# Matmul operands of a fused attention and two-MLP kernel started 4 to 56 bytes into their SBUF slots

## The chip, the cores and the metric

The kernel runs on one core of one Trainium2 chip. The metric is device time in microseconds of one execution. The kernel before takes 1527.72 us, the median of two runs (1527.64 and 1527.79 us).

## The reference

Three stages follow each other. `_attn_ref` packs 576 keys and values of each of 8 batches and 8 heads into 32 rows by a softmax attention, and lets the 576 queries attend to those 32 rows. `_moe_ref` and `_moe2_ref` are two dense MLPs over all 4608 tokens, 512 wide with 2048 hidden units.

```python
def _attn_ref(q, k, v, p):            # (8, 8, 576, 64); p has 32 rows
    p_packed = sm_attn(p, k, v)
    out = sm_attn(q, p_packed, p_packed)
    return out.astype(np.float32)

def _moe_ref(x, w_in, w_out):
    h = x @ w_in
    g = np.where(h > 0.0, h, alpha * (np.exp(np.minimum(h, 0.0)) - 1.0))
    return (g @ w_out).astype(np.float32)

def _moe2_ref(x, w_in, w_out, a, b):
    h = x @ w_in
    P = a[0] + a[1] * h + a[2] * h2 + a[3] * h3
    Q = 1.0 + np.abs(b[0]) * np.abs(h) + np.abs(b[1]) * h2
    g = P / (Q + 1e-06)
    return (g @ w_out).astype(np.float32)
```

## The kernel before

The order of the work is written out by hand, step by step, in the main loops at the end of the kernel function; the engines run their instructions in that order. There are two phases.

Phase A (lines 935 to 963) does attention and the first MLP. The tokens are taken as 8 batches of two halves of 288 tokens, and each half takes 16 steps, one for each 128 hidden units: 256 steps. The second attention isn't finished as such. Its softmax weights, transposed, are the tile `A` (two heads' rows, one half), and `m` is the packed values times the first MLP's `w_in`, so that `h` is `m` times `A`. Every number is split into a high and a low part of type float32r, and a product is taken as three matmuls (high by high, low by high, high by low). In a step, `a_h` (L358) issues 6 matmuls of 288 columns whose moving operand is a slice of `A`; ScalarE and VectorE make `g` (L376, L377, L382); `a_hi` (L387, ScalarE) and `a_lo` (L392, VectorE) split it into `ghi` and `glo`; `a_o` (L402) issues 12 matmuls whose moving operand is `ghi` or `glo`, into four accumulators. The stationary operands there are `m` and `wo`. The tile `A` is written by `s2_hi` (L311, ScalarE) and `s2_lo` (L316, VectorE) from `s2y`, which `s2_tr` (L305, VectorE) transposes. Attention of the next batch and the unpacking of the weights run between the steps. The result of the first MLP goes to DRAM (`x2d`).

Phase B (lines 966 to 999) does the second MLP over 9 blocks of 512 tokens, 16 steps each: 144 steps. `b_load` (L611, the DMAs of L616 on SP's queue) brings a block's x, high and low, as two tiles `xb` of 1 MB each; two blocks are held at a time, and a block is loaded while the one before it is worked on. In a step, `b_h` (L631) issues 12 matmuls of 512 columns whose moving operand is `xb` (stationary: the weights `w`); ScalarE and VectorE work out the rational function (L645 to L668); `b_split` makes `ghi` (L674, ScalarE) and `glo` (L676, GpSimd); `b_o` (L684) issues 12 matmuls in which `ghi` or `glo` is the stationary operand and `wo` the moving one.

Tiles come from pools with slots by tag. In the kernel before, the built program has every matmul operand, moving and stationary, at an SBUF address that is a multiple of 64 bytes.

Of the kernel before, what the change touches and what calls it, by code (L numbers as in the profile page):

```python
# [10 lines left out]
F32 = mybir.dt.float32  # L11
F32R = mybir.dt.float32r
# [10 lines left out]
def packed_attention_moe_moe2_kernel(  # L23
# [15 lines left out]
    B, _, NJ, S = qT.shape  # L39
# [5 lines left out]
    NF = DFF // 128  # L45
    NC = DFF // 512
    TA = S // 2
    NBLK = TA // 32
    TB = 512
    NTB = NT // TB  # L50
    NKD = DM // 128
# [10 lines left out]
    WI = (1, 2, 3, 4, 7, 8, 9, 10, 11, 12, 13, 14)  # L62
    SCH = (6, 8, 11, 13, 14), (18, 24), (20, 22, 26, 30)
    NWS = NF - 1

    P = ctx.enter_context(tc.tile_pool(name="P", bufs=1))
    dram = ctx.enter_context(tc.tile_pool(name="dram", bufs=1, space=bass.MemoryType.DRAM))
# [2 lines left out]
    T = actx.enter_context(tc.tile_pool(name="T", bufs=1))  # L70
# [230 lines left out]
    def s2_tr(b, hf):  # L301
        d = st[b]
        x, m = d.pop(("s2x", hf))
        y = T.tile([128, 2, TA], F32, tag="s2y", name=f"s2y_{b}_{hf}")
        nc.vector.transpose(y.rearrange("p a s -> p (a s)"), x.rearrange("p a s -> p (a s)"))  # L305
        d["s2y", hf] = y

    def s2_hi(b, hf):
        d = st[b]
        d["A", hf] = A = T.tile([128, 2, 2, TA], F32R, tag="A", name=f"A_{b}_{hf}", bufs=tag_bufs["A"])  # L310
        nc.scalar.copy(A[:, 0], d["s2y", hf])  # L311

    def s2_lo(b, hf, eng=None):
# [4 lines left out]
    tag_bufs = dict(A=3, raw=2, cvt=2, E=2, aT=2)  # L318
# [27 lines left out]
    def a_step(s):  # L346


        b, t = divmod(s, 2 * NF)
        if b == 0:  # L350
            for n, f0, f1 in RUNS:
                if t < f1 - f0:
                    return b, n, f0 + t, (t == 0, t == f1 - f0 - 1)
                t -= f1 - f0
        n, f = divmod(t, NF)
        return b, n, f, (f == 0, f == NF - 1)
# [26 lines left out]

    def a_hi(s):
        d = mlp[s]
        d["ghi"] = T.tile([128, TA], F32R, tag="ghi", name=f"ghi_{s}", bufs=2)
        nc.scalar.copy(d["ghi"], d["g"])  # L387

    def a_lo(s):
        d = mlp[s]  # L390
        d["glo"] = T.tile([128, TA], F32R, tag="glo", name=f"glo_{s}", bufs=2)
        nc.vector.tensor_tensor(d["glo"], d["g"], d["ghi"].bitcast(F32), ALU.subtract)  # L392

    acc = None
# [92 lines left out]
    def scr_open(key, tiles):  # L487
        closed.discard(key)
        scr.extend((key, t) for t in tiles)
# [119 lines left out]
    xb = {}  # L609

    def b_load(n, tags):  # L611
        ts = []
        for i in range(2):
            pool, tag = tags[i]
            t = pool.tile([128, NKD, TB], F32R, tag=tag, name=f"xb{n}_{i}")
            nc.sync.dma_start(out=t.bitcast(F32), in_=x2d[i][:, :, n * TB:(n + 1) * TB].bitcast(F32))  # L616
            ts.append(t)
        xb[n] = ts
# [18 lines left out]
    def tt(tag, s, bufs, dt=F32):  # L637
        return TBP.tile([128, TB], dt, tag=tag, name=f"{tag}_{s}", bufs=bufs)
# [30 lines left out]

    def b_split(s):  # L670
        d = bst[s]
        d["ghi"] = tt("ghi", s, 2, F32R)
        d["glo"] = tt("glo", s, 2, F32R)
        nc.scalar.copy(d["ghi"], d["g"])  # L674
        eng = nc.vector if s == NTB * NF - 1 else nc.gpsimd
        eng.tensor_tensor(d["glo"], d["g"], d["ghi"].bitcast(F32), ALU.subtract)  # L676
# [23 lines left out]
    with tc.manual_schedule():  # L700
# [16 lines left out]
        def loads(n=len(seq), x=slice(0, RW)):  # L717
            for _ in range(n):
# [3 lines left out]
                used = [x[0] for x in slot.values()]  # L722
                fs = [f for f in range(NWS) if at_seq["o", f] > i and f not in used]
                if fs:
# [27 lines left out]
        V, A = nc.vector, nc.scalar  # L752
# [15 lines left out]
        def tscr(tag, cols=512, name="scr"):  # L768
            t = T.tile([128, cols], F32, tag=tag, name=f"{name}_{tag}", bufs=tag_bufs.get(tag, 1))
            return t[:, :512]  # L770

        scr_open("t", [tscr("cvt"), tscr("cvt", name="scr2"), tscr("w"), tscr("whi")])
        for f in range(NWS, NF):
            t = P.tile([128, 2, 512], F32, tag=f"wo{f}", name=f"scr_wo{f}")
# [42 lines left out]
        s2_mul(0, 0, V)  # L817
        s2_pe(0, 1, extra("s2x"))
        s2_tr(0, 0)
        s2_hi(0, 0)  # L820
        m_lo(0, 0, half(0)[0])
        s2_lo(0, 0, V)
# [21 lines left out]
        def s2_at(s, *a):  # L844
            seq_at(s, a, (s2_pe, s2_max), s2_sub, s2_exp, s2_sum, s2_mul, s2_tr, s2_hi, s2_lo)
# [25 lines left out]
        for t, fn, *a in ((-2, m_hi, 0, 0, h1), (-2, m_lo, 0, 0, h1), (-2, c3, oo[0]), (-2, c4, oo[0], nc.gpsimd),  # L871
                          (-2, s2_max, 0, 1), (-2, s2_sub, 0, 1, V),
                          (-1, s2_exp, 0, 1), (-1, c3, oo[1]), (-1, s2_sum, 0, 1), (-1, s2_mul, 0, 1, V),
                          (-1, c4, oo[1], V),
                          (0, c3, oo[2]), (0, c4, oo[2], nc.gpsimd), (0, s2_tr, 0, 1), (0, s2_hi, 0, 1),
                          (0, s2_lo, 0, 1, V)):
            at(ewq, t, fn, *a)
        for p in seq[NKD + 1:]:
            t = when[p]
# [14 lines left out]
        for b in range(B - 1):  # L894
            o, n = b * NS, b + 1
# [25 lines left out]
        for i, piece in enumerate(pieces):  # L921
            s = NS * (1 + i // 6) + (2, 7, 12, 17, 22, 27)[i % 6]
            at(ldq, s - 4, w2_raw, piece)
            at(ewq, s, w2_up, piece)
            for k, fn in enumerate((w2_bits, w2_hi, w2_lo)):
                at(ewq, s + 1 + k, fn, piece)
        o = (B - 1) * NS
        at(ldq, o + 19, b_load, 0, ((P, "v"), (P, "k")))
        for c in range(NC):
            at(ldq, o + 3 + c, w2_load, 0, c)  # L930
# [5 lines left out]
        for s in range(-2, NA):  # L936
            if s == 0:
                prox.close()
                pacc = actx.enter_context(
                    tc.tile_pool(name="ps_acc", bufs=1, space=bass.MemoryType.PSUM, reuse_waits="tile"))  # L940
                acc = [pacc.tile([128, 512], F32, tag=f"acc{m}", name=f"acc{m}") for m in range(4)]
            run(ldq, s)
            if s + 2 < NA:
                a_h(s + 2)
            run(peq, s)
            lo = None
            if 0 <= s + 1 < NA:
                a_hi(s + 1)
                lo = functools.partial(a_lo, s + 1)
            if s + 2 < NA:  # L950
                a_act1(s + 2)
            if s in cvq:
                c1(cvq.pop(s), lo)
            elif lo:
                lo()
            if s + 2 < NA:
                a_dve1(s + 2)
            run(ewq, s)
            if s >= 0:
                a_o(s)  # L960
            if s >= 0 and a_step(s)[3][1] and a_evac(s):
                at(ewq, s + 1, a_spill, s)
# [3 lines left out]
        TBP = ctx.enter_context(tc.tile_pool(name="TB", bufs=1, reuse_waits="tile"))  # L966
# [3 lines left out]
        XT = [((P, "v"), (P, "k")), ((P, "q"), (TBP, "xb"))]  # L970
        NB = NTB * NF
        b_load(1, XT[1])
        b_h(0)
        b_act1(0)
# [4 lines left out]
        b_dve2(0)  # L979
        b_dve1(1)  # L980
        b_split(0)
        b_h(2)
        for s in range(NB):
            n, f = divmod(s, NF)
            if f == 0 and 1 <= n and n + 1 < NTB:
                b_load(n + 1, XT[(n + 1) % 2])
            if s + 3 < NB:
                b_h(s + 3)
            if s + 1 < NB:
                b_act2(s + 1)  # L990
            if s + 2 < NB:
                b_act1(s + 2)
            if s + 1 < NB:
                b_dve2(s + 1)
            if s + 2 < NB:
                b_dve1(s + 2)
            if s + 1 < NB:
                b_split(s + 1)
            b_o(s)
# [51 lines left out]
```

## Time and profile before

| | |
|---|---|
| median of two runs | 1527.72 us |
| the profiled execution, whole | 1528.13 us |
| its span, first to last instruction | 1526.4 us |
| PE busy | 1504.6 us (99%) |
| DVE busy | 1108.6 us (73%) |
| ACT busy | 1044.3 us (68%) |
| POOL busy | 188.5 us (12%) |
| DMA, mean over the span | 95 GB/s |

The span leaves out 1.7 us of the profiled execution. PE is TensorE's matmuls and PEld its weight loads, which overlap them; DVE is VectorE, ACT is ScalarE, POOL is GpSimd. A line L402 is line 402 of the kernel. Matmuls are pipelined, and the duration of one reaches into the next, so what one costs is the distance from one start to the next.

### The profile page before, as it was taken

What the parts mean: (1) busy time and instruction counts of PE and PEld (TensorE: products, weight loads), DVE (VectorE), ACT (ScalarE), POOL (GpSimd) and SP (SyncE); (2) the same over time, 40 slices, a digit from 0 to 9 for tenths busy, and PEclk for the clock granted to TensorE, in tenths of its full rate; (3) what the DMA queues carried; (4) which work ended last, traced back from release to release, by engine and by line L of the source; (5) the groups of instructions that cost most, each with busy time, mean ns of one, the idle gap of its engine ahead of it and who ended that gap; (6) DMA issues with size and microseconds to landing.
All of it is one profiled execution on the core that took longest, in us unless ns stands there. A gap on an engine that the chain in (4) does not pass through costs nothing.

```text
span 1526.4 us, 25313 instructions
## 1 busy us (share of the span) xinstructions
PE 1504.6 (99%) x9906; PEld 1307.5 (86%) x9906; DVE 1108.6 (73%) x1954; ACT 1044.3 (68%) x1965; POOL 188.5 (12%) x151
## 2 busy tenths in 40 slices
PE   7899999999999999999999999999999999999998
PEld 5788989999999989899888888888888888888887
DVE  6887676757667676644686878777786877778786
ACT  4876676766666666665676777777676777767675
POOL 0000000000000000000122222222222222222221
PEclk9999999999999999999999999999999999999999
DMA  9525434435353443035801002020200202020000
GB/s 354 177 102 189 143 102 163 147 125 171 133 162 103 146 141 111 32 142 187 316 1 54 30 2 83 1 84 0 83 1 14 70 1 83 0 83 1 28 1 28
DMA packets 64744, 144.76 MB, mean 95 GB/s; under 512 B 4849, under 2 KB 24561, under 8 KB 61809
## 3 DMA queue, kind: packets, MB, share of 16 engines
q1 hardware_dynamic: 64624, 143.15, 26.9%
q8 instruction: 77, 1.26, 0.3%
q14 instruction: 43, 0.34, 0.1%
HBM read 98.04 MB, written 45.09 MB: 94 GB/s over the span
## 4 chain that ended last, share of the span: by engine, by line
PE 94%; DVE 3%; ACT 2%; issue 1%; POOL 0%; ACTq 0%; POOLq 0%; DVEq 0%
PE accb L684 26%; PE hb L631 26%; PE acc L402 26%; PE h L367 12%; PE m L325 2%; PE pp L227 1%; PE s L261 1%; PE s1h L161 1%; PE warm L764 0%; DVE wi L481 0%; PE t L204 0%; DVE g L382 0%; DVE glo L392 0%; DVE wo L558 0%; ACT ghi L387 0%
## 5 line engine op out<-in xcount | busy, mean ns | idle before, releaser
L402 PE MATMUL acc<-ghi,wo 128*128 128x288 f32 x2048 | 458.1, 300 | 2.5 <-ACT xpart L425 1.1
L631 PE MATMUL hb<-xb,w 128*128 128x512 f32 x1728 | 414.6, 389 | 0.0
L631 PEld LDWEIGHTS hb<-xb,w 128*128 128x128 f32 x1728 | 324.3, 188 | 67.3
L402 PEld LDWEIGHTS acc<-ghi,wo 128*128 128x128 f32 x2048 | 341.8, 188 | 43.0 <-ACT g L376 19.6
L684 PE MATMUL accb<-wo,ghi 128*128 128x512 f32 x1152 | 354.7, 389 | 0.0
L676 POOL TENSOR_TENSOR glo<-g,ghi 128x512 fp32r<-128x512 f32 x143 | 185.3, 1296 | 1290.9 <-ACT ghi L674 1290.9
L402 PE MATMUL acc<-glo,wo 128*128 128x288 f32 x1024 | 302.0, 295 | 3.7 <-DVE glo L392 3.4
L684 PEld LDWEIGHTS accb<-wo,ghi 128*128 128x128 f32 x1152 | 216.3, 188 | 44.9
L367 PE MATMUL h<-A,m 128*128 128x288 f32 x1536 | 247.0, 296 | 1.9 <-DVE m L339 0.8
L684 PE MATMUL accb<-wo,glo 128*128 128x512 f32 x576 | 224.1, 389 | 0.0
L367 PEld LDWEIGHTS h<-A,m 128*128 128x128 f32 x1536 | 217.4, 188 | 3.7 <-DVE m L339 1.5
L382 DVE SCALAR_TENSOR_TENSOR g<-g,h 128x288 f32<-128x288 f32 x256 | 115.9, 453 | 115.3 <-ACT g L377 115.2
L387 ACT CAST ghi<-g 128x288 fp32r<-128x288 f32 x256 | 110.6, 432 | 127.4 <-PE acc L402 107.1
L402 PEld LDWEIGHTS acc<-glo,wo 128*128 128x128 f32 x1024 | 192.6, 188 | 5.1 <-DVE glo L392 5.1
L392 DVE TENSOR_TENSOR glo<-g,ghi 128x288 fp32r<-128x288 f32 x256 | 116.3, 454 | 81.5 <-ACT ghi L387 80.7
L665 DVE SCALAR_TENSOR_TENSOR Q<-Q,L 128x512 f32<-128x512 f32 x144 | 99.7, 692 | 102.6 <-ACT L L659 102.6
L645 ACT ACTIVATE w<-hb,ab_sb 128x512 f32<-128x512 f32 x144 | 98.4, 684 | 88.7 <-PE hb L631 88.7
L674 ACT CAST ghi<-g 128x512 fp32r<-128x512 f32 x144 | 89.8, 623 | 96.6 <-PE accb L684 62.3
L376 ACT ACTIVATE g<-h 128x288 f32<-128x288 f32 x256 | 105.1, 411 | 65.7 <-PE h L367 62.9
L684 PEld LDWEIGHTS accb<-wo,glo 128*128 128x128 f32 x576 | 108.0, 188 | 22.6
L668 DVE SCALAR_TENSOR_TENSOR g<-t,cf,Q 128x512 f32<-128x512 f32 x144 | 108.3, 752 | 17.3 <-DVE Q L666 1.4
L377 ACT ACTIVATE g<-g 128x288 f32<-128x288 f32 x256 | 113.7, 444 | 8.1
(346 smaller groups left out, 1494.9 us busy)
## 6 DMA issues: line engine op xcount, KB each, us to landing
xb<-x2d SPq DMA_DIRECT2D x18, 1024.0 KB, 7.4
x2d<-x SPq DMA_DIRECT2D x30, 576.0 KB, 3.6
out_dram<-o SPq DMA_DIRECT2D x35, 256.0 KB, 2.1
v<-in_v_dram SPq DMA_DIRECT2D x8, 1024.0 KB, 7.1
w<-wi2d SPq DMA_DIRECT2D x8, 1024.0 KB, 10.5
wo<-wo2d SPq DMA_DIRECT2D x16, 512.0 KB, 10.9
k<-in_kT_dram SPq DMA_DIRECT2D x7, 1152.0 KB, 7.2
q<-in_qT_dram SPq DMA_DIRECT2D x7, 1152.0 KB, 5.3
```

Source lines behind the costliest of these rows:

```text
L367: nc.tensor.matmul(ps[:, :TA], lhsT=m[:, wx, r, c0:c0 + 128], rhs=A[:, ax, r, :], start=(i == 0), stop=(i == 5))
L376: nc.scalar.activation(d["e"], d["h"][:, :TA], AF.Exp)
L377: nc.scalar.activation(d["e"], d["e"], AF.Relu, scale=-1.0, bias=1.0)
L382: nc.vector.scalar_tensor_tensor(d["g"], d["e"], -1.0, d["h"][:, :TA], ALU.mult, ALU.max)
L387: nc.scalar.copy(d["ghi"], d["g"])
L392: nc.vector.tensor_tensor(d["glo"], d["g"], d["ghi"].bitcast(F32), ALU.subtract)
L402: nc.tensor.matmul(acc[m][:, :TA], lhsT=w[:, wx, m * 128:(m + 1) * 128], rhs=d[g], start=(first and i == 0), stop=(last and i == 2))
L631: nc.tensor.matmul(ps, lhsT=w[:, k, c0:c0 + 128], rhs=x[:, k, :], start=(i == 0), stop=(i == 3 * NKD - 1))
L665: nc.vector.scalar_tensor_tensor(Q, Q, 1.0 + 1e-6, r, ALU.add, ALU.mult)
L668: nc.vector.scalar_tensor_tensor(d["g"], t, cf[:, 0:1], Q, ALU.add, ALU.mult)
L676: eng.tensor_tensor(d["glo"], d["g"], d["ghi"].bitcast(F32), ALU.subtract)
L684: nc.tensor.matmul(acc[m], lhsT=d[g][:, m * 128:(m + 1) * 128], rhs=w[:, wx, :], start=(f == 0 and i == 0), stop=(f == NF - 1 and i == 2))
```

## The change

Each of the tiles below gets a longer slot, and the data starts some elements of 4 bytes into it. `OFA` gives the amount for a batch in phase A, `OFB` that for a block in phase B.

| | elements | bytes |
|---|---|---|
| `OFA`, batches 0 to 7 | 0, 1, 2, 4, 8, 12, 6, 10 | 0, 4, 8, 16, 32, 48, 24, 40 |
| `OFB`, blocks 0 to 8 | 1, 2, 4, 8, 12, 6, 14, 10, 3 | 4, 8, 16, 32, 48, 24, 56, 40, 12 |

`s2y` loses its own slot and takes one of the two of `aT`.

```diff
+    OFA = [0, 1, 2, 4, 8, 12, 6, 10]
+    OFB = [1, 2, 4, 8, 12, 6, 14, 10, 3]
@@ s2_tr
-        y = T.tile([128, 2, TA], F32, tag="s2y", name=f"s2y_{b}_{hf}")
+        y = T.tile([128, 2, TA], F32, tag="aT", name=f"s2y_{b}_{hf}", bufs=tag_bufs["aT"])
@@ s2_hi
-        d["A", hf] = A = T.tile([128, 2, 2, TA], F32R, tag="A", name=f"A_{b}_{hf}", bufs=tag_bufs["A"])
+        t = T.tile([128, 4 * TA + 80], F32R, tag="A", name=f"A_{b}_{hf}", bufs=tag_bufs["A"])
+        A = d["A", hf] = t[:, OFA[b]:OFA[b] + 4 * TA].rearrange("p (i r t) -> p i r t", i=2, r=2)
@@ a_hi
-        d["ghi"] = T.tile([128, TA], F32R, tag="ghi", name=f"ghi_{s}", bufs=2)
+        o = OFA[a_step(s)[0]]
+        d["ghi"] = T.tile([128, TA + 96], F32R, tag="ghi", name=f"ghi_{s}", bufs=2)[:, o:o + TA]
@@ a_lo
-        d["glo"] = T.tile([128, TA], F32R, tag="glo", name=f"glo_{s}", bufs=2)
+        o = OFA[a_step(s)[0]]
+        d["glo"] = T.tile([128, TA + 96], F32R, tag="glo", name=f"glo_{s}", bufs=2)[:, o:o + TA]
@@ b_load
-            t = pool.tile([128, NKD, TB], F32R, tag=tag, name=f"xb{n}_{i}")
+            t = pool.tile([128, NKD * TB + 128], F32R, tag=tag, name=f"xb{n}_{i}")
+            t = t[:, OFB[n]:OFB[n] + NKD * TB].rearrange("p (k t) -> p k t", k=NKD)
@@ b_split
-        d["ghi"] = tt("ghi", s, 2, F32R)
-        d["glo"] = tt("glo", s, 2, F32R)
+        o = OFB[s // NF]
+        for x in ("ghi", "glo"):
+            d[x] = TBP.tile([128, TB + 128], F32R, tag=x, name=f"{x}_{s}", bufs=2)[:, o:o + TB]
```

In the built program the start addresses of these operands, taken modulo 64 bytes, are those of the table; all other matmul operands stay at multiples of 64 bytes. No engine's instructions change their order or their number. Which semaphores an instruction waits for differs in five rows, all in the first steps of phase B: waits for finished DMA writes stand one or two instructions earlier, because the slots of phase B lie over other slots of phase A.

## Rows read from the trace of the kernel before

**Rows 1.** The page: span, and busy time of each engine.

```profile
span 1526.4 us, 25313 instructions
PE 1504.6 (99%) x9906; PEld 1307.5 (86%) x9906; DVE 1108.6 (73%) x1954; ACT 1044.3 (68%) x1965; POOL 188.5 (12%) x151
...
PEclk9999999999999999999999999999999999999999
```

**Rows 2.** The page: the chain that ended last, by engine and line.

```profile
PE 94%; DVE 3%; ACT 2%; issue 1%; POOL 0%; ACTq 0%; POOLq 0%; DVEq 0%
PE accb L684 26%; PE hb L631 26%; PE acc L402 26%; PE h L367 12%; PE m L325 2%; PE pp L227 1%; PE s L261 1%; PE s1h L161 1%; PE warm L764 0%; DVE wi L481 0%; PE t L204 0%; DVE g L382 0%; DVE glo L392 0%; DVE wo L558 0%; ACT ghi L387 0%
```

**Rows 3.** Windows: stretch, its length, busy us of each engine, PEclk, DMA.

```profile
core 0: us, PE busy (x) PEld busy (x) DVE busy (x) ACT busy (x) POOL busy (x), PEclk, DMA share, GB/s
...
218.80:306.60 87.80, 87.80 (x798) 80.72 (x797) 60.20 (x128) 59.28 (x134) 0.00 (x0) 1.00 0.43 141
...
923.60:1010.60 87.00, 87.00 (x386) 72.03 (x385) 67.54 (x99) 62.07 (x99) 20.71 (x16) 1.00 0.10 37
...
738.50:1522.10 783.60, 783.60 (x3458) 648.40 (x3456) 610.42 (x885) 560.22 (x883) 185.29 (x143) 1.00 0.11 39
```

**Rows 4.** Chain in order of time, phase A: start us, us, what.

```profile
499.51 0.80 PE h L367 x6
500.31 1.60 PE acc L402 x12
501.91 0.80 PE h L367 x6
```

**Rows 5.** Chain in order of time, last block of phase B.

```profile
1440.46 2.72 PE accb L684 x12
1443.18 2.72 PE hb L631 x12
```

**Rows 6.** Weight loads in order of time, phase A: start us, us.

```profile
500.01 0.19 PEld L402 LDWEIGHTS acc<-ghi,wo 128*128 128x128 f32 x1
500.15 0.19 PEld L402 LDWEIGHTS acc<-glo,wo 128*128 128x128 f32 x1
```

**Rows 7.** Groups by line: count | busy us, mean ns | idle before.

```profile
L684 PEld LDWEIGHTS accb<-wo,ghi 128*128 128x128 f32 x1152 | 216.3, 188 | 44.9
...
L674 ACT CAST ghi<-g 128x512 fp32r<-128x512 f32 x144 | 89.8, 623 | 96.6 <-PE accb L684 62.3 <-DVE g L668 29.6 <-PE hb L631 4.7
```

**Rows 8.** Tile s2m on VectorE: count, ns min/median/max, first and last start.

```profile
L285 DVE TENSOR_TENSOR s2x<-s2x,s2m x16: 751/752/758, 19.0 to 636.0; 128x576 f32<-128x576 f32 x16
...
L299 DVE TENSOR_TENSOR s2x<-s2x,s2m x16: 751/752/758, 21.8 to 644.4; 128x576 f32<-128x576 f32 x16
```

**Rows 9.** SP's queue in order of time: last weight write, phase B's loads.

```profile
607.40 0.32 SPq L593 DMA_DIRECT2D wo2d<-w('o', 15)_7844  x1
...
709.22 2.04 SPq L616 DMA_DIRECT2D xb<-x2d  x2
...
750.19 1.25 SPq L616 DMA_DIRECT2D xb<-x2d  x2
...
835.05 1.23 SPq L616 DMA_DIRECT2D xb<-x2d  x2
```

**Rows 10.** Tile xb: first and last use by matmuls, and DMA landing.

```profile
L631 PE MATMUL hb<-xb,w x1728: 387/389/398, 738.5 to 1510.8; 128*128 128x512 f32 x192
...
DMA to landing us min/median/max: 5.3/7.4/11.5
```

## The prediction

> **What bounds the kernel now.** I read the page first, then the chain, then the windows by stage, and only then single instructions. The page says that TensorE is busy for 1504.6 of 1526.4 us, with VectorE and ScalarE at about 70% and GpSimd at 12% [rows 1]. A busy TensorE can still be one that waits inside its pipeline, so the chain is the better witness: 94% of it is TensorE, and 90% belongs to the four lines of the two MLPs, L684, L631, L402 and L367 [rows 2]. The windows show the same by stage. Phase B lasts 783.6 us with TensorE busy in all of it; the stretch of 87.8 us of one batch of phase A is full too. [...]
>
> So the time is a count of matmuls times the distance between their starts. In phase A 12 matmuls of 288 columns take 1.60 us and 6 take 0.80 us: 133.3 ns each [rows 4]. In phase B 12 matmuls of 512 columns take 2.72 us, whichever of the two lines: 226.7 ns each [rows 5]. The difference, 93.3 ns for 224 columns, is 0.417 ns per column. 288 columns by that rate are 120.0 ns and 512 are 213.3 ns; at both widths 13.3 ns are left. A matmul here costs its columns and a constant of 13.3 ns, though the work beside it and the roles of the operands differ between the phases. Check by count: 9 blocks x 16 steps x 24 matmuls = 3456, times 226.7 ns = 783.4 us, against the window's 783.6. Phase B has no gap in it at all. Phase A has 256 steps x 18 = 4608 matmuls, times 133.3 ns = 614.4 us; the rest of that phase is attention, which the change leaves where it is.
>
> **What the change touches.** It adds no instruction, takes none away and moves none. It alters addresses. On TensorE, the moving operand starts off its old grid of 64 bytes in batches 1 to 7 (7 x 32 steps x 18 = 4032 matmuls of L367 and L402) and in all of L631 (144 x 12 = 1728): 5760 matmuls. The stationary operand does in all of L684: 1728 more. Batch 0 starts where it did. On the other engines the writers of these tiles (L311, L316, L387, L392, L674, L676) and the DMAs of `xb` write to shifted addresses. `s2y` takes over a slot of `aT`.
>
> **Moving operands, 5760 matmuls.** The trace of before has no matmul with a shifted operand, so the price is bounded. From below: at most the constant goes, 13.3 ns x 5760 = 76.8 us, if it is something that the old addresses cause. From above: shifted data makes each of these matmuls pay the constant a second time, +76.8 us; a halved rate for a part of them is a rival below. Neither end is likely for these reasons. The constant is the same at 288 and at 512 columns, for `A`, `ghi`, `glo` and `xb` as moving operands, in slots at different places; it looks like a cost of changing from one matmul to the next and not of where data begins. And the nearest rows in which the same instruction reads an operand at two phases cost the same: L285 and L299 read the 18 values per partition of `s2m`, the one from the start of the tile and the other 72 bytes in, that is, by the addresses of the built program, at 0 or 32 and at 8 or 40 bytes beyond a multiple of 64. Both take 752 ns at the median [rows 8]. That is VectorE and a small operand, but it is the row that bears most on the question. I price a shifted read at between nothing, as there, and one column more, 0.417 ns, as a row of numbers that no longer fits its units of storage may need one unit more: 0 to 5760 x 0.417 = 2.4 us. Nothing in the rows splits these, so I take the middle, +1.2 us.
>
> [...]
>
> **Stationary operands, 1728 matmuls.** A weight load lasts 188 ns [rows 7] and runs under the matmul before it. In phase A loads of that length start 0.13 to 0.14 us apart [rows 6], so they overlap each other and the engine can start one about every 133 ns. In phase B a matmul comes only every 226.7 ns. A shifted load may take 226.7 - 133.3 = 93.4 ns more before TensorE waits. Cost taken: 0; from below 0, since a load that is off the path has nothing to give; from above, a doubled start distance, 2 x 133.3 = 266.6 ns, which exceeds 226.7 by 39.9 ns: 1728 x 39.9 = 69 us.
>
> **Writers.** ScalarE is busy for 62.1 us and VectorE for 67.5 us of the 87.0 us of a block [rows 3], 16 steps. That leaves 1.6 and 1.2 us per step. The cast L674 takes 0.62 us [rows 7]; even at twice its time ScalarE stays below TensorE. The cover is TensorE's 5.44 us per step; without it a doubled cast would cost 144 x 0.62 = 89 us. A batch of phase A has 28 us of its 87.8 free on either engine [rows 3]. Cost taken: 0.
>
> **DMAs.** The first two tiles `xb` are issued at 709.2 to 711.3 us [rows 9]; a load of `xb` lands within 11.5 us at the most [rows 10], and the first matmul that reads it starts at 738.5 us [rows 10]. That leaves 738.5 - 711.3 - 11.5 = 15.7 us. Later blocks have far more: issued at 750.2 and 835.1 us [rows 9], each is needed a block after, 87.0 us on. Slower writes to shifted addresses stay hidden up to more than twice the present landing time. Cost taken: 0.
>
> [...]
>
> **`s2y`.** The slot that it takes was last read by the matmuls of L227 of the same or the previous batch, which stand long before it in the order; no wait is added on VectorE. The few waits that stand earlier at the start of phase B are for DMA writes of the unpacked weights, the last of which is issued at 607.4 us [rows 9], 131 us before that phase. Cost taken: 0.
>
> **The sum.** The profiled execution's 1526.4 us of span + 1.2 us = 1527.6; the 1.7 us outside the span make 1529.3. The median of the runs lies 0.4 us below the profiled execution (1527.72 against 1528.13), so the forecast is 1528.9 us. A kernel like this one can be told from no change at about 2%, 30.6 us; I forecast no difference.
>
> **Rivals.**
>
> *A second start.* A moving operand off its grid makes the read start twice, so each such matmul pays the 13.3 ns again, because TensorE has no gap to hide it in. If all starts off 64 bytes pay, it is 76.8 us: 1604.5 us. If only those off 16 bytes do (batches 1, 2, 6, 7 and blocks 0, 1, 5, 6, 7, 8: 4 x 576 + 6 x 192 = 3456 matmuls), it is 46.1 us: 1573.8 us. It decides from 30.6 us / 5760 = 5.3 ns per matmul. For it speaks that every matmul sits on the path; against it, rows 8. [...] Chance 0.13.
>
> *Pairs that straddle.* At 0.417 ns per column TensorE takes 4 bytes per partition each time. If its port delivers two columns at once, and only in pairs that start at multiples of 8 bytes, then shifts of 4 and 12 bytes halve the rate: batch 1 (576 matmuls) and blocks 0 and 8 (384). 576 x 120.0 ns + 384 x 213.3 ns = 69.1 + 81.9 = 151 us: 1678.7 us. [...] Chance 0.06.
>
> *Weights become the bound.* The doubled distance between loads from above: +69 us, 1596.7 us, in L684 alone. Against it, the margin of 93.4 ns. Chance 0.04.
>
> *The old grid is the cost.* Tiles that all start at multiples of 64 bytes make the two reads of TensorE meet in the same part of the memory, and the 13.3 ns are that meeting. Shifts of the moving operand undo it: 1527.7 - 76.8 = 1450.9 us. Against it, the constant does not vary between operands and phases. Chance 0.05.
>
> **How the numbers follow.** The forecast has 0.72. Slower by over 2% is 0.13 + 0.06 + 0.04 = 0.23, faster is 0.05, within 2% is 0.72. The likeliest case's own range is 1525 to 1531 us: the 0 to 2.4 us of the moving operands, or as much the other way. For 8 in 10 it must reach the larger version of the second start and the weights: 1525 to 1605 us leaves out the straddling pairs and the gain, 0.11, and some of the edges.
>
> **What would show it.** If I am right, 12 matmuls of L631 and of L684 still take 2.72 us and 12 of L402 1.60 us in every batch and block, and a batch lasts 87.8 us whatever its shift. A second start shows as 1.76 us for 12 matmuls of L402 and 2.88 us for 12 of L631, batch 0 being unchanged and L684 too. Straddling pairs show in batch 1 and blocks 0 and 8 alone. A weight bound shows in L684 alone. Any block in which 12 matmuls take a different time from those of batch 0 or of before makes the forecast's step on moving operands wrong; a gap on TensorE at 738 us makes the step on DMAs wrong.

## The result, and the profile after

The changed kernel takes 1549.56 us (two runs, 1549.21 and 1549.91), the kernel before 1527.72 us. The ratio is 1.0143, with a 95% interval of 1.0099 to 1.0187. That is slower by 21.8 us: less than the 2% that the forecast set as its bound, but well clear of nothing. The time lies inside the stated range of 1525 to 1605 us, 20.7 us above the predicted 1528.9 and outside the likeliest case's own range of 1525 to 1531.

The page of the changed kernel, with the lines that answer to [rows 1, 2]:

```profile
span 1547.4 us, 25313 instructions
PE 1526.5 (99%) x9906; PEld 1312.4 (85%) x9906; DVE 1109.7 (72%) x1954; ACT 1044.7 (68%) x1965; POOL 172.4 (11%) x151
...
PEclk9999999999999999999999999999999999999999
...
PE 94%; DVE 3%; DMA 1%; ACT 1%; issue 0%; SPq 0%; ACTq 0%; DVEq 0%
```

TensorE's busy time has grown by 21.9 us and the span by 21.0 us, with the same instructions. VectorE and ScalarE work as long as before, and the chain is still TensorE's. So the time is neither a wait nor a busier helper: the matmuls themselves take longer. The windows say where. Their columns are those of [rows 3].

```profile
core 0: us, PE busy (x) PEld busy (x) DVE busy (x) ACT busy (x) POOL busy (x), PEclk, DMA share, GB/s
...
219.60:308.90 89.30, 89.30 (x798) 82.25 (x797) 60.42 (x128) 59.40 (x133) 0.00 (x0) 1.00 0.42 139
308.90:395.60 86.70, 86.70 (x797) 79.67 (x797) 60.09 (x128) 59.22 (x133) 0.00 (x0) 1.00 0.42 143
395.60:483.40 87.80, 87.80 (x798) 80.76 (x796) 60.13 (x129) 59.30 (x134) 0.00 (x0) 1.00 0.41 141
...
739.40:1543.10 803.70, 803.70 (x3458) 650.67 (x3456) 611.35 (x885) 560.16 (x883) 169.10 (x143) 1.00 0.10 38
```

The last row is phase B: 803.7 us against 783.6 [rows 3], so 20.1 of the 21.0 us are there, at the same granted clock of 1.00. The three rows above are batches 2, 3 and 4 of phase A, shifted by 8, 16 and 32 bytes. They take 89.3, 86.7 and 87.8 us against 87.8 before: the 8 bytes cost and the 16 bytes gain. Over all of phase A gains and losses nearly cancel.

The chain of the changed kernel in order of time, in block 0 (4 bytes) and block 2 (16 bytes):

```profile
770.72 2.87 PE hb L638 x12
...
952.31 2.79 PE accb L692 x12
```

Twelve matmuls of L638 take 2.87 us and twelve of L692 2.79 us, where both took 2.72 [rows 5]. The weight loads are still 188 ns each and are issued under earlier matmuls, as before [rows 7]:

```profile
L692 PEld LDWEIGHTS accb<-wo,ghi 128*128 128x128 f32 x1152 | 216.7, 188 | 50.9
```

Below, "12 in 2.72" means 12 matmuls of one line in 2.72 us, read from rows of this kind.

### The profile page after: what moved, and what is told of

It reads as the page before. It is cut to its first block, busy times and chain, and to the rows that moved or that the text cites. A ratio compares the mean times of both kernels' runs of the same rounds, so it can differ in the third digit from the quotient of the medians.

```text
span 1547.4 us, 25313 instructions
## 1 busy us (share of the span) xinstructions
PE 1526.5 (99%) x9906; PEld 1312.4 (85%) x9906; DVE 1109.7 (72%) x1954; ACT 1044.7 (68%) x1965; POOL 172.4 (11%) x151
## 4 chain that ended last, share of the span: by engine, by line
PE 94%; DVE 3%; DMA 1%; ACT 1%; issue 0%; SPq 0%; ACTq 0%; DVEq 0%
PE hb L638 26%; PE accb L692 26%; PE acc L408 25%; PE h L371 12%; PE m L329 2%; PE pp L230 1%; PE s L264 1%; DMA raw0('i', 0, 0)_89<-in_w_in_dram 1%; PE s1h L164 1%; DMA raw0('i', 0, 3)_95<-in_w_in_dram 0%; DMA raw0('i', 1, 0)_114<-in_w_in_dram 0%; DVE wi L487 0%; DVE g L386 0%; PE t L207 0%; DVE glo L398 0%
## 5 line engine op out<-in xcount | busy, mean ns | idle before, releaser
L638 PE MATMUL hb<-xb,w 128*128 128x512 f32 x1728 | 425.4, 395 | 0.0
L638 PEld LDWEIGHTS hb<-xb,w 128*128 128x128 f32 x1728 | 325.9, 189 | 76.2
L692 PE MATMUL accb<-wo,ghi 128*128 128x512 f32 x1152 | 360.9, 394 | 0.0
L684 POOL TENSOR_TENSOR glo<-g,ghi 128x512 fp32r<-128x512 f32 x143 | 169.1, 1183 | 1328.7 <-ACT ghi L682 1328.7
L692 PEld LDWEIGHTS accb<-wo,ghi 128*128 128x128 f32 x1152 | 216.7, 188 | 50.9
L692 PE MATMUL accb<-wo,glo 128*128 128x512 f32 x576 | 226.9, 394 | 0.0
L682 ACT CAST ghi<-g 128x512 fp32r<-128x512 f32 x144 | 89.5, 622 | 102.7 <-PE accb L692 41.3
L692 PEld LDWEIGHTS accb<-wo,glo 128*128 128x128 f32 x576 | 108.2, 188 | 25.5
```

The costliest lines, as they stand in the source:

```text
L638: nc.tensor.matmul(ps, lhsT=w[:, k, c0:c0 + 128], rhs=x[:, k, :], start=(i == 0), stop=(i == 3 * NKD - 1))
L692: nc.tensor.matmul(acc[m], lhsT=d[g][:, m * 128:(m + 1) * 128], rhs=w[:, wx, :], start=(f == 0 and i == 0), stop=(f == NF - 1 and i == 2))
```

## The experiments

The first four undo the change in parts. Three theories stood at the start: where operands begin is what costs; the moved slots cost; and one shifted stream upsets the matmuls after it too.

**Longer slots alone.**

```diff
-    OFA = [0, 1, 2, 4, 8, 12, 6, 10]
-    OFB = [1, 2, 4, 8, 12, 6, 14, 10, 3]
+    OFA = [0] * 8
+    OFX = [0] * 9
+    OFG = [0] * 9
...
```

`OFX` takes the place of `OFB` for x of phase B, `OFG` for its `ghi` and `glo`.

> All shifts are zero here; the longer slots and the move of s2y stay. Theory S (where an operand starts is what costs): the time of the kernel before, 1527.7 us within 2 us, 12 matmuls of a line of phase B in 2.72 us. Rival L (the slots that moved are what costs, as their tiles now lie otherwise to each other): 1549 us, 12 matmuls in 2.79 us.

Measured: 1529.41 us, ratio 1.0011, interval 1.0000 to 1.0023. Its chain in phase B:

```profile
951.58 2.72 PE accb L693 x12
```

The moved slots are not the cause; what is left of the change is where the operands start. Some 1.7 us stay, at the edge of the noise, as the interval begins at 1.0000. They lie in phase A, where a full batch takes 88.0 us for 87.8 by the windows, and where the places of `ghi` and `glo` relative to `wo` changed with the slots; the fifth experiment shows that such places count there.

**Only x of phase B.** `OFX` keeps the nine shifts of `OFB`; `OFA` and `OFG` are zero.

> Only the x of phase B is shifted, the moving operand of L638. In the changed kernel L638 takes 6.1 ns and L692 5.5 ns more per matmul than before. Theory S with separate costs: L638 keeps its 6 ns, L692 goes back to 226.7 ns, 1527.7 + 1728 x 6.1 ns = 1538 us. Rival (one shifted stream upsets the pace of all that follows): both lines slow, about 1547 us.

Measured: 1543.57 us, ratio 1.0103, interval 1.0074 to 1.0133. That lies between the two expectations. Block 0, by the chain:

```profile
770.55 2.85 PE hb L639 x12
773.40 2.77 PE accb L693 x12
```

L639, whose x is shifted, has 12 in 2.85. L693 has nothing shifted and still takes 2.77. The timeline of one such run of L693 (start us, length us, and how many) tells why:

```profile
773.24 0.63 PE L693 MATMUL accb<-wo,ghi 128*128 128x512 f32 x2
...
773.94 0.62 PE L693 MATMUL accb<-wo,ghi 128*128 128x512 f32 x2
...
774.63 0.62 PE L693 MATMUL accb<-wo,ghi 128*128 128x512 f32 x2
...
775.32 0.62 PE L693 MATMUL accb<-wo,ghi 128*128 128x512 f32 x2
...
776.00 1.35 PE L639 MATMUL hb<-xb,w 128*128 128x512 f32 x5
```

From start to start, three matmuls each, these are 0.70, 0.69, 0.69 and 0.68 us. The unshifted line begins slow, after the slow line before it, and only comes back to 226.7 ns for its last matmuls. Then the shifted line starts again. The expectation that both lines would be fully slow is wrong; that they have separate costs is wrong too. The groups of the unshifted line, first in the kernel before and then here (busy us, mean ns, idle us), show that it pays 582.3 - 578.8 = 3.5 of the 14.2 us by which this kernel is slower than the one with longer slots alone:

```profile
L684 PE MATMUL accb<-wo,ghi 128*128 128x512 f32 x1152 | 354.7, 389 | 0.0
...
L684 PE MATMUL accb<-wo,glo 128*128 128x512 f32 x576 | 224.1, 389 | 0.0
```

```profile
L693 PE MATMUL accb<-wo,ghi 128*128 128x512 f32 x1152 | 357.1, 391 | 0.0
...
L693 PE MATMUL accb<-wo,glo 128*128 128x512 f32 x576 | 225.2, 391 | 0.0
```

**Only ghi and glo of phase B.** `OFG` keeps the shifts; `OFA` and `OFX` are zero.

> Only ghi and glo of phase B are shifted, the stationary operand of L692. Theory S with separate costs: L638 at 226.7 ns, L692 about 232 ns, 1527.7 + 1728 x 5.5 ns = 1537 us. Rival (one shifted stream upsets the pace of all that follows): about 1547 us. If a weight load hides what a shift costs it: 1528 us, and the 232 ns of L692 came from L638.

Measured: 1537.90 us, ratio 1.0066, interval 1.0043 to 1.0089, which is the time of the first expectation (1537). The weight loads do not hide the shift of a stationary operand. Block 0 (4 bytes) and block 2 (16 bytes):

```profile
770.39 2.75 PE hb L639 x12
773.14 2.78 PE accb L693 x12
```

```profile
943.74 2.72 PE accb L693 x12
946.46 2.72 PE hb L639 x12
```

As the stationary operand, 4 bytes cost and 16 bytes cost nothing. So there is no price per shifted operand as such. In block 0 the unshifted L639 is slow as well (2.75): the time of the first expectation came out, its separate costs did not.

**Only phase A.** `OFA` keeps the shifts; `OFX` and `OFG` are zero.

> Only phase A is shifted. By the batches of the changed kernel, where batches 1 and 2 (4 and 8 bytes) take 1.3 to 1.5 us more and batch 3 (16 bytes) 1.0 us less than before: 1528.5 us, with the same batches slow and fast. Rival (the differences between batches are chance): other batches slow and fast.

Measured: 1529.18 us, ratio 1.0009, interval 0.9997 to 1.0020, against the 1529.41 us of the longer slots alone: the shifts of phase A give and take in sum nothing. As expected, the same batches are slow and fast: by the windows, batches 1, 2 and 3 take 89.5, 89.3 and 86.7 us, as in the changed kernel. Batch 3 has again its 12 matmuls of 288 columns in 1.56 us (133.3 ns each were 1.60):

```profile
344.14 1.56 PE acc L409 x12
```

The parts add up to a little more than the whole: 14.2 us for x (1543.57 - 1529.41), 8.5 for `ghi` and `glo`, -0.2 for phase A, 1.7 for the slots are 24.2, against 21.8. The rest fits the pace that one line hands to the other, which is paid once when both are shifted: with `ghi` and `glo` alone shifted L639 is busy for 416.5 us against 414.6 before, but on top of shifted x this adds next to nothing (425.2 us with x alone, 425.4 in the changed kernel). No run tested it by itself.

**16 bytes in all of phase A.** `OFA = [4] * 8`, phase B not shifted.

> A, ghi and glo of phase A start 16 bytes in, in all batches; phase B is not shifted. If the 86.7 us of batch 3 in the changed kernel belong to the 16 bytes, every full batch takes 86.7 us against 88.0 with the longer slots alone: 1529.4 - 7.5 x 1.3 = 1520 us, faster than the kernel before by 0.5%. Rival (they belong to what else runs in batch 3, or to the change of shift between batches): 1528 to 1530 us.

Measured: 1519.05 us against 1528.10 us of the kernel before in the same runs, ratio 0.9938, interval 0.9922 to 0.9955: faster than both kernels, and the first expectation (1520). Phase A and phase B of this run:

```profile
343.30 1.56 PE acc L409 x12
...
952.72 2.72 PE accb L693 x12
```

So the 13.3 ns that a matmul costs beyond its columns aren't a constant. By the addresses of the built program, `ghi` and `glo` lie 64 and 192 bytes from `wo`, modulo 256, in the kernel before, 128 with the longer slots, and 144 here.

**Is it the distance?** In phase B of the kernel before, that distance is 0 for every matmul. This made theory P: the distance between the two operands, modulo 256, sets the pace. Its rival A is a price for each operand's own place on a grid of 64 bytes. Here the weights are shifted as well; phase A isn't, and its slots have their old lengths, which makes room.

```diff
+    OFW = 4
+    OFB = [4, 0, 4, 8, 4, 12, 4, 2, 4]
...
-        t = P.tile([128, NKD, 512], F32R, tag=("wi", "m")[i] + str(c), name=f"w2_{i}_{c}")
+        t = P.tile([128, NKD * 512 + 16], F32R, tag=("wi", "m")[i] + str(c), name=f"w2_{i}_{c}")
+        t = t[:, OFW:OFW + NKD * 512].rearrange("p (k x) -> p k x", k=NKD)
...
-        t = P.tile([128, 2, 512], F32R, tag=f"wo{f}", name=f"wo2_{f}")
+        t = P.tile([128, 2 * 512 + 16], F32R, tag=f"wo{f}", name=f"wo2_{f}")
+        t = t[:, OFW:OFW + 2 * 512].rearrange("p (i x) -> p i x", i=2)
```

> In phase B the weights of the second MLP start 16 bytes in, and x, ghi and glo 16, 0, 16, 32, 16, 48, 16, 8 and 16 bytes in, in blocks 0 to 8; phase A is not shifted. Theory P (the pace depends on where the moving and the stationary operand of one matmul begin relative to each other): blocks 0, 2, 4, 6 and 8 at 226.7 ns per matmul, 87.04 us, the others at 88 to 89.5 us; in all about 1536 us. Rival A (each operand pays for its own distance from the grid of 64 bytes): all blocks at 88.5 to 90 us, only block 1 less; in all about 1547 us.

Measured: 1542.71 us, ratio 1.0093, interval 1.0073 to 1.0113; all blocks slow, block 0 for instance:

```profile
773.16 2.78 PE hb L641 x12
```

It decides nothing: each slot of the weights had grown by 64 bytes, so the weights lay at four places modulo 256, and one block mixed four distances. Later runs repeat it without this flaw.

**A sweep of x.** `OFA = [0, 3, 5, 7, 9, 11, 13, 15]`, `OFX = [16, 32, 64, 128, 5, 7, 9, 11, 13]`, `OFG` zero.

> Only moving operands are shifted: in phase A by 0, 12, 20, 28, 36, 44, 52 and 60 bytes in batches 0 to 7, in phase B x by 64, 128, 256, 512, 20, 28, 36, 44 and 52 bytes in blocks 0 to 8. Theory P and rival A alike: blocks 0 to 3, whose shifts are multiples of 64 bytes, at 87.04 us, as before, the others at 88 to 89.5 us; in phase A between 86.5 and 89.5 us per batch. If a larger grid than 64 bytes mattered, blocks 0 to 2 would differ from block 3.

Measured: 1539.75 us (one run). The chain in blocks 0, 1, 2 and 3 (64, 128, 256 and 512 bytes), then 4 and 5 (20 and 28 bytes):

```profile
769.58 2.76 PE hb L639 x12
...
869.12 2.79 PE hb L639 x12
...
962.20 2.72 PE hb L639 x12
...
1038.36 2.72 PE hb L639 x12
...
1132.16 2.84 PE hb L639 x12
...
1220.65 2.74 PE hb L639 x12
```

Both theories missed: 64 and 128 bytes cost, 256 and 512 don't, which is the larger grid that the last sentence of the expectation allowed for. The grid of x against its weights is 256 bytes, not 64. Blocks 6, 7 and 8 (36, 44 and 52 bytes), and 12 bytes, in block 8 of the kernel with x alone shifted:

```profile
1303.54 2.82 PE hb L639 x12
...
1392.18 2.76 PE hb L639 x12
...
1480.92 2.83 PE hb L639 x12
```

```profile
1490.72 2.75 PE hb L639 x12
```

Of the small shifts 28 bytes cost least (2.74) and, with the 4 bytes of block 0 above (2.85), this has a pattern of 16: starts 4 bytes past a multiple of 16 are the dearest (4, 20, 36, 52), those 12 bytes past it the cheapest (12, 28, 44). Phase A of this run has the same order. Batches 3, 4 and 5 are shifted by 28, 36 and 44 bytes, and a batch takes 88.0 us unshifted with these slots:

```profile
core 0: us, PE busy (x) PEld busy (x) DVE busy (x) ACT busy (x) POOL busy (x), PEclk, DMA share, GB/s
...
307.30:393.90 86.60, 86.60 (x796) 79.59 (x795) 60.04 (x129) 59.09 (x134) 0.00 (x0) 1.00 0.42 143
393.90:483.00 89.10, 89.10 (x797) 82.03 (x796) 60.46 (x129) 59.49 (x134) 0.00 (x0) 1.00 0.41 139
483.00:569.70 86.70, 86.70 (x798) 79.69 (x797) 60.15 (x129) 59.25 (x134) 0.00 (x0) 1.00 0.43 143
```

So shifts of 28 and 44 bytes cost a little in phase B and gain in phase A.

**Everything 32 bytes later.** The kernel before, with one small tile ahead of all others.

```diff
+    first = P.tile([128, 8], F32, tag="first", name="first")
+    nc.vector.memset(first, 0.0)
     ident = P.tile([128, 128], F32, tag="ident", name="ident")
```

> The kernel before with one tile of 32 bytes (and one memset of it) placed ahead of all others, so that every tile of the kernel starts 32 bytes later and keeps its distance to every other. Theory P (the distance between the moving and the stationary operand, taken modulo 256 bytes, sets the pace; in phase B of the kernel before it is 0): 1527.7 us within 2 us, 226.7 ns per matmul in phase B. Rival A (each operand pays for its own distance from a grid of 64 bytes, which all operands now leave by 32): phase B slower by 5 to 6 ns per matmul, about 1546 us.

Measured: 1527.75 us against 1527.71, ratio 0.9999, interval 0.9988 to 1.0011.

```profile
947.67 2.72 PE hb L633 x12
950.39 2.72 PE accb L686 x12
```

All operands have left the grid of 64 bytes and nothing happened: rival A falls. A shift of x by 32 bytes alone, in block 3 of the kernel with x shifted, costs:

```profile
1037.01 2.80 PE hb L639 x12
```

**Multiples of 16 for x.** `OFA = [4] * 8`, `OFX = [20, 24, 28, 36, 40, 44, 48, 52, 60]`, `OFG` zero.

> Phase A as in e5_a_16_bytes; in phase B x is shifted by 80, 96, 112, 144, 160, 176, 192, 208 and 240 bytes in blocks 0 to 8, all multiples of 16; ghi and glo are not shifted. Theory P: each of these distances has a pace of its own between 226.7 and 234 ns for L638, the first matmuls of L692 after each change of line too, phase B at 792 to 800 us and the whole at 1528 to 1536 us; a distance with a pace below 226.7 ns would be a faster phase B. Rival (a block's time is chance): no order in it. By the sweep of 12 to 60 bytes no shift of x in phase B came below 226.7.

Measured: 1533.48 us (one run), within the 1528 to 1536 us of theory P. Phase B was slow in all nine blocks, 192 bytes among them; 96 bytes, in block 1, for example:

```profile
854.52 2.81 PE hb L639 x12
```

No distance came below 2.72, so the kernel before has the best start for phase B that was tried.

**A common shift of 16, and of 4 bytes.** The slots of the second MLP's `w` grow by 256 bytes here, so that all its weights have one place. Phase A has its old slots again. In the first kernel the weights start 16 bytes in, and x as below; in the second `OFW = 1` and `OFX = [1, 1, 1, 1, 65, 0, 2, 5, 3]`.

```diff
+    OFA = [0] * 8
+    OFW = 4
+    OFX = [4, 4, 4, 4, 68, 0, 8, 5, 3]
+    OFG = [0] * 9
...
-        t = P.tile([128, NKD, 512], F32R, tag=("wi", "m")[i] + str(c), name=f"w2_{i}_{c}")
+        t = P.tile([128, NKD * 512 + 64], F32R, tag=("wi", "m")[i] + str(c), name=f"w2_{i}_{c}")
+        t = t[:, OFW:OFW + NKD * 512].rearrange("p (k x) -> p k x", k=NKD)
```

> The test of e6_pairs without its flaw (there the slots of the weights grew by 64 bytes, so that weights lay at four places modulo 256): here those slots grow by 256 bytes, the weights of L638 all start 16 bytes in, ghi, glo and the weights of L692 and phase A aren't shifted. x starts 16 bytes in in blocks 0 to 3, 272 in block 4, and 0, 32, 20 and 12 in blocks 5 to 8. Theory P (only the distance counts, modulo 256 bytes): blocks 0 to 4 at 226.7 ns for L638 and 87.04 us, blocks 6 to 8 at 88 to 89.6 us. Rival G (both the distance and where on a grid of 32 or 64 bytes the rows start): blocks 0 to 4 slow as well, 230 to 233 ns for L638.

Measured: 1537.36 us (one run). Block 0, where both operands are 16 bytes in, and block 5, where only the weights are:

```profile
769.03 2.76 PE hb L641 x12
...
1198.21 2.72 PE hb L641 x12
```

Block 5 is free although its distance is not 0, which theory P does not allow either.

> As e10_w_16, with the weights of L638 4 bytes in; x starts 4 bytes in in blocks 0 to 3, 260 in block 4, and 0, 8, 20 and 12 in blocks 5 to 8. Theory P: blocks 0 to 4 at 226.7 ns for L638 and 87.04 us. Rival G (a row that starts off the units of 16 bytes costs by itself): blocks 0 to 4 slow, towards the 238 ns that 4 bytes cost in e2_x_only.

Measured: 1548.84 us (one run). Block 0, where both are 4 bytes in:

```profile
769.04 2.85 PE hb L641 x12
```

Theory P falls too, as the whole story: distance 0 is slow when both operands are 16 bytes off (2.76) and slower when both are 4 bytes off (2.85, no better than with x alone shifted by 4). Both things count, as rival G had it: the distance (64 and 128 bytes cost with every start on a multiple of 64), and where the rows themselves begin (a common shift of 32 bytes is free, of 16 or 4 is not). The 32 bytes moved every tile, the 16 and 4 only x and its weights; 32 bytes for these two alone were not run.

## Why the prediction was right or wrong

The reading of the kernel was right: one path through TensorE, a price per matmul times a count, no wait in phase B. It is why a few nanoseconds of a matmul showed in full.

That the time lies in the stated range is luck. The range reached beyond 1531 us only for the second start and the doubled weight loads, and neither is what happened; "no difference of 2%" came true because prices of up to 12 ns for some matmuls, nothing for others and gains in phase A happened to add up to 21.8 us. By the prediction's own sign, blocks whose 12 matmuls take another time than before, its step on moving operands is wrong.

*Moving operands* is the step that failed. It priced a shifted read at 0 to 0.417 ns, by VectorE's rows [rows 8], and took 1.2 us in sum. x alone cost 14.2 us, 3.5 of them in the line that wasn't shifted. Phase B's matmuls went from 226.7 to 238 ns at 4 bytes, to 228 at 28 and to 233 at 32, and no single column more explains that: the 0.417 ns, for one unit of storage more, were the author's estimate, and no run shows them. The reason that the step gave, that the 13.3 ns come from changing matmuls and not from where data begins, was wrong for a part of them: the fifth experiment took 3 ns away with 16 bytes. The rows of TensorE that it rested on agree with each other, but in all of them both operands start on multiples of 64 bytes, so they could not tell what another start costs. VectorE's two equal rows are of another engine, and what they show did not carry over to TensorE.

*Stationary operands* failed as well: cost taken 0, measured 8.5 us alone, 1.9 of them in the unshifted L639. The step argued that a weight load has 93.4 ns to spare. The loads still take 188 ns and still run ahead, and the pace changed all the same. Time to spare on the load's side did not cover it, because what changed was the distance between matmul starts and not the load's length.

*Writers*, *`s2y`* and *the slots*: nothing was taken, and the longer slots with the moved `s2y` cost 1.7 us, at the edge of the noise, in phase A's matmuls.

*DMAs* were right. x landed as fast as before (first fence, us to landing: 11.2 at the longest, 11.5 before [rows 10]), and L638 never stood idle (second fence, the page: busy us, mean ns, idle us before it):

```profile
DMA to landing us min/median/max: 5.1/7.4/11.2
```

```profile
L638 PE MATMUL hb<-xb,w 128*128 128x512 f32 x1728 | 425.4, 395 | 0.0
```

*The rivals.* "A second start" had the right direction, slower, and the wrong mechanism. It foresaw 46.1 us if only starts off 16 bytes paid and 76.8 if all off 64 did. In fact 32 and 48 bytes pay in phase B and not in phase A, 16 bytes gain in phase A, and the prices reach from -3 to +12 ns instead of 13.3. "Straddling pairs" named 4 and 12 bytes. Of these 4 is the dearest shift, but at 11 ns of 227 and not at a halved rate, and starts 12 bytes past a multiple of 16 are the cheapest of the small ones. "Weights become the bound" named the line L684, which did pay, but its loads stayed at 188 ns and the cost was not 69 us. "The old grid is the cost" was true of phase A in a small part, where 16 bytes gain 9 of its 76.8 us; in phase B no start that was tried is better than the old one.

The costs of the small shifts of x repeat every 16 bytes: 12 matmuls take 2.82 to 2.85 us at 4, 20, 36 and 52 bytes and 2.74 to 2.76 at 12, 28 and 44. That does not make multiples of 16 free: 32 bytes cost 12 x 6.7 ns. The pace depends on both places together: x at 64 or 128 bytes from its weights is slow (2.76 and 2.79) and at 256 it is not (2.72), and x shifted by 32 bytes is slow alone (2.80) and not when all tiles move with it (2.72). Whether the two reads are what gets in each other's way, no run shows.

What the hardware does in those nanoseconds stays open. The runs show that the start addresses set the pace, not by what mechanism, and no one rule here gives every price: whether the reads meet in parts of the memory or the two sequences lock to each other could not be told apart.

## What to carry to other kernels

Where TensorE is the path and each matmul loads new weights, as here, the start addresses of its two operands are a parameter of the kernel: they moved this one between 1519.05 and 1549.56 us. In phase B nothing that was tried beat both operands at the same place modulo 256, on a multiple of 32 bytes (12 in 2.72). Phase A doesn't follow that rule: there operands 64, 128 and 192 bytes apart ran at 133 ns, and 16 bytes more on the moving operand brought 130. So try a few shifts rather than trust one grid; the runs have only float32r matmuls of 288 and 512 columns. Many shifts can be measured in one run by giving each block its own and reading 12 matmuls from the chain.

## What the runs showed of the hardware that was not expected

The pace did not change at once with the line. After a shifted line, the unshifted line of the kernel with x alone shifted needed some nine of its 12 matmuls, in the run of block 0 shown above (0.70, 0.69, 0.69 and 0.68 us for three each), to come back to 226.7 ns.

GpSimd's subtraction that writes `glo` became faster at some shifts. In the kernel with `ghi` and `glo` alone shifted, 12 of them take 13.15 us in block 0 (4 bytes) and 15.53 us in block 2 (16 bytes), 1.10 against 1.29 us each. The windows of that line:

```profile
core 0: us, DVE busy (x) POOL busy (x), PEclk, DMA share, GB/s
760.00:825.00 65.00, 0.00 (x0) 13.15 (x12) 1.00 0.00 1
935.00:1000.00 65.00, 0.00 (x0) 15.53 (x12) 1.00 0.00 1
```

The 0.2 us stand in every block of the changed kernel too: at 4, 8, 24, 40 and 56 bytes it takes 1.09 to 1.10 us, at 12, 16, 32 and 48 it takes 1.29 to 1.30, as slow as unshifted (1.30 in the kernel before). It is off the path here and changed no time, and the matmuls do not follow it: in the blocks of 40 and of 32 bytes, with the fast and the slow subtraction, 12 matmuls of L693 take 2.72 and 2.79 us.
